# Block attention with top-1 experts on one core: level sums turned, level values kept, rows of x in a line, and gathers in smaller pieces

## The chip, the core and the metric

The kernel runs on one core of a Trainium2 chip. Its engines are TensorE (PE in the profile, with its weight loads as PEld), VectorE (DVE), ScalarE (ACT), GpSimd (POOL) and SyncE (SP), beside 16 DMA engines; each engine works through its own instructions in order. The metric is the time of one execution on the device in microseconds (us); several are taken and their median is given.

## The reference

Attention is computed inside chunks of 64 positions, for 8 batches with 8 heads and 576 positions of 64 values. The heads of a position side by side are a row x of 512 values, which makes 4608 rows ("tokens"). Each token goes to the one expert of eight with the largest gate logit; where an expert has more than `capacity` (80) tokens, those with the highest gate weight are kept; all others give zero.

```python
# q, k, v: (8, 8, 576, 64) float32; w_gate (512, 8); w1 (8, 512, 1024); w2 (8, 1024, 512)
scores = scale * matmul(q_c, k_c.T)              # per chunk of 64 positions
attn = exp(scores - max); attn /= sum + 1e-9
x = matmul(attn, v_c)                            # -> (4608, 512)
logits = x @ w_gate
expert_idx = argmax(logits, axis=1)
gate_w = softmax(logits)[arange(N), expert_idx]
out = zeros((N, D))
for e in range(8):
    tok_idx = where(expert_idx == e)[0]
    if len(tok_idx) > capacity:
        gw = gate_w[tok_idx]
        tok_idx = tok_idx[argpartition(-gw, capacity)[:capacity]]
    h = maximum(x[tok_idx] @ w1[e], 0.0)
    out[tok_idx] = gate_w[tok_idx, None] * (h @ w2[e])
```

## The kernel before

**Attention.** The tokens are 36 tiles (`rt`) of 128. For each, TensorE makes scores, transposes and values, VectorE and ACT the softmax, and x is written by POOL's queue to a scratch in DRAM (`xs`, L486 to L494). The gate's logits follow four tiles at a time.

**Gating.** `gate` (L543) finds the chosen expert as a one-hot row (`comp`, part 0) and the gate weight at that expert (`keys`, 128 tokens x 36 tiles x 8 experts, zero elsewhere). In `parts` POOL adds the token's number in two pieces and its key in three. The capacity's threshold comes from counts: a coarse search (`bounds`, L734) gives each expert a lower bound and a step, and 256 levels stand above it. `levels` (L601) makes (key − bound) × scale and its maximum `bo`, one number for each token; a matrix `lv` of 128 tokens x 256 levels then tells which levels lie under it. ACT makes some of the matrices (`signs`, L618), VectorE and POOL the others (`steps_`, L623). TensorE sums them by expert into `tot` (`total`, L763, `total_last`, L769): the one-hot rows are loaded and 256 columns stream, so `tot` has 8 partitions. `threshold` (L798) counts the levels that reach the capacity (`jkt`, with an accumulator) and turns the count into a threshold for each expert with one float32 matmul (`pn`). The order of the last operations on VectorE is written out by hand as a string, `LAST`: "a" steps tiles 28 to 31, "b" tiles 32 to 35, "c" two matrices on VectorE, "s" two on ACT.

**Slots.** From L1033 on: `mask` compares keys with thresholds, a scan numbers the kept tokens on each partition, TensorE makes their place (`pos`), `hot` (L807) makes a one-hot matrix for each tile (VectorE eight tiles at a time, `pk`, ACT one in nine), and 36 matmuls compact the kept tokens into `cand`. `rank` and `select` (L1080, L1086) order the candidates of each expert on VectorE into 96 slots; `place` (L162) moves row numbers to slots on TensorE. Slots make six rounds of 128 rows, each four groups of 32; a group belongs to one expert. `gic` holds the row numbers as integers, `targets` (L173) the output rows. `keep_warm` (L828) gives TensorE matmuls with no use (`pwarm`) where it has nothing else to do.

**Experts.** `experts` (L189) gathers rounds 0, 1 and 2 from `xs` with POOL (128 rows of 2 KB each), and transposes them on TensorE (`xpose`, L201) with copies by ACT; rounds 3 to 5 are gathered as quarters of rows (`quarters`, L213) and transposed by VectorE (`xpose_blocks`). `layer1` (L230) makes half a round at a time, two groups of 32 matmuls; `layer2` (L248) a round. Weights of 2 MB a layer and expert come on SP's queue; that of expert 3's first layer is held by a VectorE copy from `si` (L1162), the next ones likewise by others (`part`, `ahead`, L1155).

## Time and profile before

| | |
|---|---|
| median of 3 runs | 235.34 us (235.11 to 235.88) |
| the profiled execution's own time | 235.19 us |
| span of that execution | 233.4 us |
| mean granted TensorE clock | 0.993 |
| PE busy | 218.1 us (93 %) |
| DVE busy | 130.5 us (56 %) |
| DMA | 84.81 MB, 363 GB/s |

The profile counts from the start of the span. Attention and the gating that is interleaved with it go on until about 125 us; slots are worked out until 142; expert layers follow to 227, and the last scatter ends it. A row of a timeline tells when a group of equal instructions started, how long it took, and in brackets how long the engine had been idle before and what it had waited for.

### The profile page before, as it was taken

The numbers are of one execution on the slowest core, as the hardware profiler recorded it, in microseconds if no ns is written. First come the engines' busy times: TensorE is split into PE (matmuls) and PEld (weight loads), VectorE is DVE, ScalarE is ACT, GpSimd is POOL, SyncE is SP. The second block draws the span as 40 slices with busy tenths as digits, with TensorE's granted clock in tenths as the row PEclk, the third lists the DMA queues.
The fourth block names the chain that finished last, engine by engine and source line by source line (L and its number), as shares of the span: only waits on it lengthen the run. The fifth ranks groups of instructions, "written<-read, shape, count | busy, mean of one in ns | idle before, by whom it ended". The sixth has DMA issues, their size and how long they took to land. (4 is left out here: it accounts for less than half of the span.)

```text
span 233.4 us, 8196 instructions
## 1 busy us (share of the span) xinstructions
PE 218.1 (93%) x3513; PEld 139.2 (60%) x3513; DVE 130.5 (56%) x411; ACT 73.9 (32%) x161; POOL 66.4 (28%) x145
## 2 busy tenths in 40 slices
PE   7788999999898999999998899999999999999980
PEld 5567787877777787878864555653544536354320
DVE  6678687878779798878878874211131222203110
ACT  3124433343445636566584601321110201101000
POOL 9001203030303019392640823005124060311101
PEclk9999999999999999999999999999999999999997
DMA  6999999999999999998999976999999999999011
GB/s 214 357 406 392 409 422 418 418 421 416 420 411 409 365 409 387 391 405 320 369 437 395 404 274 219 343 423 432 407 406 427 431 409 419 435 421 388 23 46 38
DMA packets 16697, 84.81 MB, mean 363 GB/s; under 512 B 2768, under 2 KB 2896, under 8 KB 12304
## 3 DMA queue, kind: packets, MB, share of 16 engines
q1 hardware_dynamic: 12848, 71.84, 76.6%
q0 software_dynamic: 3664, 12.32, 13.7%
q8 instruction: 30, 0.49, 0.8%
q10 hardware_dynamic: 144, 0.07, 0.1%
q14 instruction: 11, 0.09, 0.1%
HBM read 64.03 MB, written 20.45 MB: 362 GB/s over the span
## 5 line engine op out<-in xcount | busy, mean ns | idle before, releaser
L237 PE MATMUL hc<-w,xtc 128*32 128x256 f32 x768 | 42.8, 379 | 0.2 <-ACT xtc L210 0.2
L254 PE MATMUL yc<-w,htc 128*32 128x512 f32 x384 | 42.1, 592 | 0.0
L406 PE MATMUL s<-kz,qv 128*64 128x128 f32 x544 | 37.2, 279 | 0.9 <-DMA qv<-in_qv 0.9
L237 PEld LDWEIGHTS hc<-w,xtc 128*32 128x32 f32 x768 | 24.7, 110 | 18.3 <-issue 2.4
L442 ACT ACTIVATE pT<-pt 128x512 f32<-128x512 f32 x36 | 21.4, 594 | 36.8 <-PE pt L440 36.7
L406 PEld LDWEIGHTS s<-kz,qv 128*64 128x64 f32 x544 | 29.0, 136 | 6.6 <-issue 6.1
L422 DVE TENSOR_REDUCE mx<-s 128x8 f32<-128x512 f32 (+1 forms) x37 | 24.9, 674 | 11.7 <-PE s L406 11.5
L254 PEld LDWEIGHTS yc<-w,htc 128*32 128x32 f32 x384 | 12.5, 110 | 26.6 <-issue 25.7
L465 PEld LDWEIGHTS o<-qv,pT 64*64 64x64 f32 x1120 | 19.9, 134 | 13.1 <-issue 9.8
L242 ACT ACTIVATE hsc<-hc 128x512 f32<-128x512 f32 x12 | 7.2, 597 | 62.9 <-PE hc L237 62.9
L465 PE MATMUL o<-qv,pT 64*64 64x65 f32 x1120 | 24.9, 224 | 2.2 <-DMA qv<-in_qv 1.1
L244 DVE STREAM_TRANSPOSE htc<-hsc 128x512 f32<-128x512 f32 x12 | 8.5, 711 | 30.1 <-ACT hsc L242 30.1
L259 DVE TENSOR_SCALAR ysc<-yc,gatec 128x512 f32<-128x512 f32 x6 | 4.5, 751 | 36.5 <-PE yc L254 27.4
L424 DVE TENSOR_TENSOR sm<-s,mx 128x512 f32<-128x512 f32 (+1 forms) x37 | 24.7, 668 | 0.1
L484 DVE TENSOR_TENSOR x<-o,rc 128x512 f32<-128x512 f32 x35 | 24.1, 690 | 0.8
L440 PE MATMUL pt<-ct,sm 128*128 128x128 f32 x144 | 23.5, 286 | 0.1
L502 PE MATMUL px<-ct,x 128*128 128x128 f32 x136 | 20.5, 273 | 0.0
L503 ACT COPY xT<-px 128x512 f32<-128x512 f32 x32 | 18.6, 580 | 0.0
L580 POOL TENSOR_TENSOR comp<-comp,ct 128x32 bf16<-128x32 bf16 x18 | 3.9, 237 | 50.4 <-DVE rc L479 40.8
L440 PEld LDWEIGHTS pt<-ct,sm 128*128 128x128 f32 x144 | 15.2, 141 | 2.7 <-DVE sm L424 0.3
L502 PEld LDWEIGHTS px<-ct,x 128*128 128x128 f32 x136 | 15.9, 141 | 0.8 <-issue 0.8
L263 POOL DMA_INDIRECT out<-ysc,si x6 | 6.0, 997 | 30.9 <-DVE ysc L259 20.2
(205 smaller groups left out, 230.9 us busy)
## 6 DMA issues: line engine op xcount, KB each, us to landing
w<-in_w SPq DMA_DIRECT2D x12, 2048.0 KB, 21.7
qv<-in_qv SPq DMA_DIRECT2D x14, 1032.0 KB, 10.6
kz<-in_kh SPq DMA_DIRECT2D x34, 256.0 KB, 10.3
xs<-x POOLq DMA_DIRECT2D x8, 1024.0 KB, 11.0
w<-in_w SPq DMA_DIRECT2D x8, 1024.0 KB, 7.8
out<-zero SPq DMA_DIRECT2D x8, 1024.0 KB, 29.0
qv<-in_qv SPq DMA_DIRECT2D x2, 520.0 KB, 9.6
qv<-in_qv SPq DMA_DIRECT2D x2, 516.0 KB, 9.4
```

The costliest lines, as they stand in the source:

```text
L237: nc.tensor.matmul(h[32 * c:32 * c + 32, j, :], lhsT=xT[r][:, g, b, :], rhs=w[:, b, 256 * c:256 * c + 256], start=(b == 0), stop=(b == 3), ...
L244: nc.vector.transpose(t.rearrange("p j b n -> p (j b n)"), a)
L254: nc.tensor.matmul(y[o:o + 32, :], lhsT=hT[r, g // 2][:, g % 2, c, :], rhs=getw(groups[r][g])[1][:, c, :], start=(c == 0), stop=(c == 7), ...
L406: nc.tensor.matmul(o, lhsT=a, rhs=b, start=True, stop=True)
L422: nc.vector.tensor_reduce(m8, s8, axis=AX.X, op=ALU.max)
L424: d['sub'] = lambda: nc.vector.tensor_tensor(d8, s8, to, op=ALU.subtract)
L440: nc.tensor.transpose(pt[:, pr, :], sv[:, pr, :], ident)
L442: nc.scalar.activation(pT, pt, AF.Exp, scale=0.125)
L465: nc.tensor.matmul(po[h][64 * u:64 * u + 64, 65 * pr:65 * pr + 65], lhsT=d['pT'][64 * h:64 * h + 64, pr, 64 * u:64 * u + 64], rhs=TT[T, r] ...
L484: nc.vector.tensor_tensor(x8, pov[..., 0:64], to, op=ALU.mult)
L502: nc.tensor.transpose(pm[:, pr, :], t['x'][:, r, P * pr:P * pr + P], ident)
L503: copy(t['xT'][:, :, P * r:P * r + P], pm)
```

## The change

1. **Turned sums.** `tot` now has 128 levels on the partitions: each matrix `lv` is loaded in two halves and the 8 columns of the one-hot rows stream. The compare in `threshold` is 16 wide, and its result goes through two bf16 matmuls with ones: the number of levels reached, on every partition. The POOL operations that prepared the scale, and `cnt` and `scale`, are gone.
2. **Kept level values.** (key − bound) × scale is kept for all tiles (`bva`, ordered by expert, then tile), and the mask compares these with the counted level. For the last four tiles `bo` is made from the gate weight and two sums over the one-hot row, beside the key. Matrix 28 moves to ACT and 30 to POOL.
3. **Rows in a line.** Row 128 × tile + partition of `xs`; the last four tiles write with four transfers instead of eight. `targets` turns the number into the output's row with more VectorE operations and stands behind `giq`.
4. **One-hots.** VectorE's steps have 8, 8, 8, 4 and 4 tiles, with four tiles on ACT; the buffers come from other tags, and no warm-up stands behind the last group.
5. **First gather.** Rank, selection and placing of round 0 in two halves of 64 rows, two gathers, and two sets of transposes, the second between the first two groups of layer 1. The gate on the first layer's weights of expert 3 is a POOL memset behind the gather of round 1.
6. **Round 2** is gathered in quarters and transposed by VectorE (`NQ` is 2).

On VectorE, the end of gating, from the matrix of tile 28 (L625) to the mask, before:

```order
L625 TENSOR_SCALAR lv_2494<-io_b,bo 128x256
L593 TENSOR_REDUCE mw_2456<-wt_2453 128x4
L625 TENSOR_SCALAR lv_2497<-io_b,bo 128x256
L594 TENSOR_TENSOR comp<-wt_2453,mw_2456 128x4x8
L596 TENSOR_REDUCE gg_2457<-ex_89 128x4
L597 RECIPROCAL gg_2457<-gg_2457 128x4
L571 TENSOR_TENSOR keys<-comp,gg_2457 128x32
L610 TENSOR_TENSOR bv_2503<-keys,lob 128x32
L613 TENSOR_TENSOR bv_2503<-bv_2503,inw 128x32
L615 TENSOR_REDUCE bo<-bv_2503 128x4
L625 TENSOR_SCALAR lv_2516<-io_b,bo 128x256
```

The same place after:

```order
L636 TENSOR_REDUCE mw_2444<-wt_2441 128x4
L637 TENSOR_TENSOR comp<-wt_2441,mw_2444 128x4x8
L639 TENSOR_REDUCE gg_2445<-ex_87 128x4
L640 TENSOR_TENSOR sw<-comp,ofs 128x64
L643 RECIPROCAL gg_2445<-gg_2445 128x4
L644 TENSOR_REDUCE s_2447<-sw 128x8
L610 TENSOR_TENSOR keys<-comp,gg_2445 128x32
L646 TENSOR_TENSOR gm_2443<-gg_2445,s_2447 128x4
L647 TENSOR_TENSOR bva<-keys,low 128x4x8
L649 TENSOR_TENSOR bo<-gm_2443,s_2447 128x4
L650 TENSOR_TENSOR bva<-bva,ofs 128x4x8
L687 TENSOR_SCALAR lv_2521<-io_b,bo 128x256
```

Two matrices have left the chain, and `bo` no longer comes from the level values.

On VectorE, the first ranks (`bt`, with `rk`), selections and row numbers (`gic`), before:

```order
L1074 TENSOR_REDUCE kc<-s_112 128x8
L1082 SCALAR_TENSOR_TENSOR bt_2648,rk<-kr_2636,kc,ct 128x128
L1082 SCALAR_TENSOR_TENSOR bt_2650,rk<-kr_2636,kc,ct 128x128
L1088 TENSOR_SCALAR sel_2652<-io_b,rk 128x96
L1088 TENSOR_SCALAR sel_2654<-io_b,rk 128x96
L1082 SCALAR_TENSOR_TENSOR bt_2656,rk<-kr_2639,kc,ct 128x128
L170 TENSOR_REDUCE gic_2663<-pl_2658 128x1
L1082 SCALAR_TENSOR_TENSOR bt_2668,rk<-kr_2639,kc,ct 128x128
L1088 TENSOR_SCALAR sel_2670<-io_b,rk 128x96
```

And after:

```order
L1137 TENSOR_REDUCE kc<-s_110 128x8
L1145 SCALAR_TENSOR_TENSOR bt_2659,rk<-kr_2647,kc,ct 128x128
L1151 TENSOR_SCALAR sel_2661<-io_b,rk 128x96
L1177 TENSOR_REDUCE gic_2664<-pl_2663 64x1
L1145 SCALAR_TENSOR_TENSOR bt_2668,rk<-kr_2647,kc,ct 128x128
L1151 TENSOR_SCALAR sel_2670<-io_b,rk 128x96
L1177 TENSOR_REDUCE gic_2664<-pl_2663 64x1
L1145 SCALAR_TENSOR_TENSOR bt_2677,rk<-kr_2650,kc,ct 128x128
L1145 SCALAR_TENSOR_TENSOR bt_2682,rk<-kr_2650,kc,ct 128x128
L1151 TENSOR_SCALAR sel_2684<-io_b,rk 128x96
```

One reduce over placed rows now stands behind each of the first two selections, ahead of the next rank.

On TensorE, from the last spread matmul to the first layer, before (`xpc`, transposes of a gathered round; `hc`, layer 1):

```order
L1126 MATMUL acc<-parts_2712,spread 128x6
L833 MATMUL pwarm<-ct 128x512
L208 MATMUL xpc_0_2793<-ct,xgc_2774 128x128 x2
L208 MATMUL xpc_2_2797<-ct,xgc_2774 128x128 x2
L237 MATMUL hc_0_2801<-w_0_491,xtc_2792 32x256 x32
L208 MATMUL xpc_0_2839<-ct,xgc_2778 128x128 x4
L237 MATMUL hc_1_2845<-w_0_491,xtc_2792 32x256 x16
```

And after:

```order
L1200 MATMUL acc<-parts_2726,spread 128x8
L899 MATMUL pwarm<-ct 128x512
L225 MATMUL xpc0a<-ct,xgc0a 128x64 x4
L270 MATMUL hc_0_2836<-w_0_487,xtc_2829 32x256 x16
L225 MATMUL xpc0b<-ct,xgc0b 128x64 x4
L270 MATMUL hc_0_2836<-w_0_487,xtc_2829 32x256 x16
L270 MATMUL hc_1_2879<-w_0_487,xtc_2829 32x256 x16
L238 MATMUL xpc_0_2897<-ct,xgc_2802 128x128 x4
```

The first transposes have half the columns, the second half of them stands behind the first group of layer 1, and those of round 1 behind the third group.

The diff, cut to what is spoken of:

```diff
-NQ = 3
+NQ = 2
+STORE = 3
...
-LAST = "aaaaaabababasbcbcbbbbbbb"
+LAST = "aaaaaabababasbbbbbbbbbbbb"
...
+        def gather_half(h):
+            t = pool.tile([P, DM], F32, name=f"xg{tag}0{'ab'[h]}", tag="xg", bufs=4)[0:64]
+            nc.gpsimd.indirect_dma_start(
+                out=t, out_offset=None, in_=xs[:, :],
+                in_offset=bass.IndirectOffsetOnAxis(ap=gi(0)[0:64, h:h + 1], axis=0),
+                bounds_check=NT * 512 - 1, oob_is_err=False)
+            xg[0, h] = t
+
+        def xpose_half(h):
+            if h == 0:
+                xT[0] = pool.tile([P, 4, P], F32, name=f"xt{tag}0", tag="xt").rearrange(
+                    "p b (g t) -> p g b t", g=4)
+            pm = pp.tile([P, 4, 64], F32, name=f"xp{tag}0{'ab'[h]}", tag="hp" if h else "xp",
+                         bufs=2 if h else 1)
+            for b in range(4):
+                nc.tensor.transpose(
+                    pm[:, b, :], xg[0, h].rearrange("p (m b) -> p b m", b=4)[:, b],
+                    ident[0:64, 0:64])
+            nc.scalar.copy(xT[0][:, 2 * h:2 * h + 2].rearrange("p g b t -> p b g t"),
+                           pm.rearrange("p b (g t) -> p b g t", g=2))
...
-        for r in range(NQ if extra else 2):
-            gather(r)
         if extra:
+            gather_half(0)
+            gather_half(1)
+            gather(1)
+            extra(-1, xg)
+            quarters(2, None)
             extra(0, xg)
-        xpose(0)
+            xpose_half(0)
+        else:
+            gather(0)
+            gather(1)
+            xpose(0)
         for r in range(NR + 1):
+            start = extra and r == 0
             if r < NR:
-                layer1(r, 0)
-            if r + 1 < (NQ if extra else NR):
+                layer1(r, 0, (lambda: xpose_half(1)) if start else None)
+            if r + 1 < NR and not extra:
                 xpose(r + 1)
             if r < NR:
-                layer1(r, 1)
+                layer1(r, 1, (lambda: xpose(1)) if start else None)
             if extra and NQ <= r + 1 < NR:
                 xpose_blocks(r + 1)
-            if extra and NQ <= r + 2 < NR:
+            if extra and NQ < r + 2 < NR:
...
-                for c in range(2):
-                    r0 = (2 * r + c) * 576 + 512
-                    nc.gpsimd.dma_start(xs[r0:r0 + 64, :], t['x'][64 * c:64 * c + 64, r, :])
+                nc.gpsimd.dma_start(xs[P * i:P * i + P, :], t['x'][:, r, :])
...
+            if rt == RT - 4:
...
+                        lambda: v.tensor_reduce(g, ex, axis=AX.X, op=ALU.add),
+                        lambda: v.tensor_tensor(
+                            sw, oh[:, :, None, :].to_broadcast([P, n, 2, NE]),
+                            ofs[:, None].to_broadcast([P, n, 2, NE]), op=ALU.mult),
+                        lambda: v.reciprocal(g, g),
+                        lambda: v.tensor_reduce(s2, sw, axis=AX.X, op=ALU.add),
+                        key,
+                        lambda: v.tensor_tensor(m, g, s2[:, :, 0], op=ALU.mult),
+                        lambda: v.tensor_tensor(b, kk, low[:, None, :].to_broadcast(bc),
+                                                op=ALU.subtract),
+                        lambda: v.tensor_tensor(bo[:, sl], m, s2[:, :, 1], op=ALU.subtract),
+                        lambda: v.tensor_tensor(b, b, ofs[:, None, 0].to_broadcast(bc),
+                                                op=ALU.mult)):
+                    queue.append((fn, ()))
+                return
             for fn in (
...
-            tot = S['tot'] = ps1.tile([NE, 2 * P], F32, name="tot", tag="pt")
-            nc.tensor.matmul(tot, lhsT=sums, rhs=S['acc'], start=True, stop=False)
-            nc.tensor.matmul(tot, lhsT=nsign, rhs=ones_b[:, 0:1].to_broadcast([P, 2 * P]),
+            tot = S['tot'] = ps1.tile([P, 2, NE], F32, name="tot", tag="pt")
+            for h in range(2):
+                nc.tensor.matmul(tot[:, h], lhsT=S['acc'][:, P * h:P * h + P], rhs=sums,
+                                 start=h == 0, stop=False)
+            nc.tensor.matmul(tot, lhsT=ones_b, rhs=nsign[:, None, :].to_broadcast([P, 2, NE]),
                              start=False, stop=False)
...
-                nc.tensor.matmul(S['tot'], lhsT=comp[:, j, 0], rhs=U[j]['lv'],
-                                 start=False, stop=j == RT - 1)
+                for h in range(2):
+                    nc.tensor.matmul(S['tot'][:, h], lhsT=U[j]['lv'][:, P * h:P * h + P],
+                                     rhs=comp[:, j, 0], start=False,
+                                     stop=h == 1 and j == RT - 1)
...
-            jk = gk.tile([P, 2 * P], BF16, name="jkt", tag="lv", bufs=LV)
-            nc.vector.tensor_scalar(jk[0:NE], S['tot'], capc[0:NE], None, op0=ALU.is_ge,
-                                    op1=ALU.add, accum_out=cnt[0:NE])
+            ge = gk.tile([P, 2, NE], BF16, name="ge", tag="ge", bufs=1)
+            nc.vector.tensor_scalar(ge, S['tot'], capc, None, op0=ALU.is_ge)
             pn = ps2.tile([P, NE], F32, name="pn", tag="g")
-            nc.tensor.matmul(pn, lhsT=cnt.to_broadcast([40, P]), rhs=scale, start=True, stop=True)
+            for h in range(2):
+                nc.tensor.matmul(pn, lhsT=ones_b, rhs=ge[:, h], start=h == 0, stop=h == 1)
...
-            for w, rt in (("a", 28), ("b", 32)):
-                levels(tails[w], rt, 4)
+            levels(tails["a"], 28, 4)
             total()
             total_last(range(20, 28))
             keep_warm(3)
-            tails["c"].extend((steps_, (nc.vector, j)) for j in (28, 30))
             for w in LAST:
                 if w == "s":
-                    signs(29)
-                    signs(31)
+                    steps_(nc.gpsimd, 30)
+                    for j in (29, 31, 28):
+                        signs(j)
                 else:
                     step_one(tails[w])
-            total_last((29, 28, 31, 30))
+            total_last((29, 31, 30, 28))
             keep_warm(3)
...
-                mask, keys.rearrange("p r e -> p e r"),
+                mask, bva,
...
-            for b0, others in ((0, "a"), (9, "a"), (18, "a"), (27, "a")):
-                n = 9 - len(others)
+            for b0, n, b1 in ((0, 8, 8), (9, 8, 17), (18, 8, 26), (27, 4, 31), (32, 4, None)):
                 hot(b0, "v", n)
-                for j, way in enumerate(others):
-                    hot(b0 + n + j, way, 1)
-                order += range(b0, b0 + 9)
+                order += range(b0, b0 + n)
+                if b1:
+                    hot(b1, "a", 1)
+                    order.append(b1)
...
-                if rt % 9 == 8:
+                if rt in (8, 17, 26):
...
-            for e in (0, 1):
-                rank(e)
-            for e in (0, 1):
-                select(e)
+            rank(0)
+            select(0)
+            pl0 = ps2.tile([P, 2, 5], F32, name="pl0", tag="g")
+            gi0 = mp.tile([P, 2], I32, name="gic0")
+
+            def place_first(groups, h):
+                for g in groups:
+                    for o, c in ((32 * g, 0), (32 * g - 64, 1))[:1 + h]:
+                        nc.tensor.matmul(pl0[o:o + 32, c], lhsT=sel_part(*divmod(g, 3)),
+                                         rhs=cb[:, :, g // 3], start=True, stop=True,
+                                         tile_position=(0, o))
+                with nc.allow_low_precision(reason="row numbers are whole and far below 2^24"):
+                    nc.vector.tensor_reduce(gi0[0:64, h:h + 1], pl0[0:64, h, 0:2], axis=AX.X,
+                                            op=ALU.add)
+            place_first((0, 1), 0)
+            rank(1)
+            select(1)
+            place_first((2, 3), 1)
             rank(2)
-            pl0, gi0 = place(mp, ps2.tile([P, 1, 5], F32, name="pl0", tag="g"), sel_part, cb, "c", 0, 1)
             keep_warm(18)
...
-            pt = ps2.tile([P, NE], F32, name="ptot", tag="g")
+            pt = ps1.tile([P, NE], F32, name="ptot", tag="pt")
...
+            gate, sv = targets(mp, [(pl0[:, 0:1], gi0[:, 0:1]), (pl1, gi1)], "c")
+            nc.vector.tensor_tensor(sv, sv, slot_oob, op=ALU.add)
+            si = mp.tile([P, NR], I32, name="si")
+            nc.vector.tensor_scalar(fl, fl, 2 * BIG, None, op0=ALU.mult)
+            nc.vector.tensor_scalar(si, sv, fl, None, op0=ALU.add)
...
+                    if after is True:
+                        nc.gpsimd.memset(w[l][:, 0, 0:1], 0.0)
...
-                if r < 5:
+                if r < 0:
+                    part(3, 0, True)
+                    clear(3.5, nc.sync, 2)
+                elif r < 5:
```

## Rows read from the trace of the kernel before

**Rows 1.** Stretches: window, length, busy us (count) by engine, PE clock, DMA share, GB/s

```profile
136.00:142.20 6.20, 5.98 (x48) 2.83 (x46) 5.56 (x42) 0.53 (x3) 2.96 (x3) 1.00 0.48 163
142.20:226.80 84.60, 84.49 (x1160) 38.28 (x1160) 15.80 (x23) 8.62 (x16) 17.84 (x21) 1.00 0.88 358
...
206.00:216.00 10.00, 10.00 (x164) 5.12 (x160) 2.08 (x3) 1.19 (x2) 0.98 (x1) 1.00 0.95 398
216.00:226.80 10.80, 10.75 (x103) 2.99 (x92) 0.75 (x1) 0.00 (x0) 0.98 (x1) 1.00 0.09 33
```

**Rows 2.** Timeline of VectorE, end of the gate: start us, us, engine, line, operation

```profile
125.00 0.18 DVE L593 TENSOR_REDUCE mw<-wt 128x4 f32<-128x32 f32 x1
125.10 0.28 DVE L625 TENSOR_SCALAR lv<-io_b,bo 128x256 bf16<-128x256 bf16 x1
125.29 0.18 DVE L594 TENSOR_TENSOR comp<-wt,mw 128x32 bf16<-128x32 f32 x1
...
126.72 0.68 DVE L625 TENSOR_SCALAR lv<-io_b,bo 128x256 bf16<-128x256 bf16 x3
```

**Rows 3.** Timeline of VectorE, threshold and mask

```profile
127.87 0.47 DVE L801 TENSOR_SCALAR_CACHE_REDUCE jkt<-tot,capc 8x256 bf16<-8x256 f32 x1 [0.47 <-PE tot L776]
...
128.82 0.69 DVE L1035 TENSOR_TENSOR mask<-keys,pn 128x288 bf16<-128x288 f32 x1 [0.48 <-PE pn L804]
```

**Rows 4.** Groups by line and shape: softmax subtraction on VectorE, busy us and mean ns

```profile
L424 DVE TENSOR_TENSOR sm<-s,mx 128x512 f32<-128x512 f32 x35 | 23.9, 682 | 0.1
```

**Rows 5.** Timeline of VectorE and TensorE, one-hots and the last compaction matmuls

```profile
131.24 2.95 DVE L811 TENSOR_TENSOR pk<-io_h,ptok_b 128x1024 bf16<-128x1024 bf16 x4
134.30 0.64 PE L1062 MATMUL s<-comp,pk 128*128 128x40 bf16 x9
```

**Rows 6.** Timeline of VectorE and TensorE, first ranks, selections and places

```profile
135.69 0.35 DVE L1082 SCALAR_TENSOR_TENSOR bt<-kr,kc,ct 128x128 bf16<-128x128 f32 x1 [0.53 <-PE kr L1100]
136.24 0.40 DVE L1088 TENSOR_SCALAR sel<-io_b,rk 128x96 bf16<-128x96 bf16 x2
136.14 0.59 PE L833 MATMUL pwarm<-io_b,ones_b 128*128 128x512 bf16 x2
136.67 0.20 PE L166 MATMUL pl<-cb,sel 128*32 128x5 bf16 x4
136.91 0.16 DVE L170 TENSOR_REDUCE gic<-pl 128x1 int32<-128x2 f32 x1
136.99 0.34 DVE L1082 SCALAR_TENSOR_TENSOR bt<-kr,kc,ct 128x128 bf16<-128x128 f32 x1
137.25 0.24 DVE L1088 TENSOR_SCALAR sel<-io_b,rk 128x96 bf16<-128x96 bf16 x1
```

**Rows 7.** Timeline of all engines, first gather to the first layer 1

```profile
137.36 1.15 POOL L195 DMA_INDIRECT xgc<-xs,gic  x1 [2.97 <-DVE bt L1082]
...
140.34 0.17 PEld L1126 LDWEIGHTS <-spread 128*128 128x128 bf16 x4 [0.25 <-DVE rowc L182]
...
140.98 0.20 PEld L208 LDWEIGHTS xpc<-ct,xgc 128*128 128x128 f32 x1 [0.24 <-DMA xgc<-xs,gic]
...
141.41 0.64 PE L208 MATMUL xpc<-ct,xgc 128*128 128x128 f32 x4
...
141.83 0.65 ACT L210 COPY xtc<-xpc 128x256 f32<-128x256 f32 x2 [1.82 <-PE xpc L208]
...
142.26 3.66 PE L237 MATMUL hc<-w,xtc 128*32 128x256 f32 x64 [0.22 <-ACT xtc L210]
```

**Rows 8.** Timeline of TensorE, transposes inside the first layer 1

```profile
145.85 0.75 PE L208 MATMUL xpc<-ct,xgc 128*128 128x128 f32 x4
```

**Rows 9.** Timeline of POOL, four level matrices, and the last transfer of x

```profile
101.23 4.52 POOL L625 TENSOR_SCALAR lv<-io_b,bo 128x256 bf16<-128x256 bf16 x4
...
128.03 0.53 POOL L489 DMA_DIRECT2D xs<-x  x1 [6.94 <-DMA xs<-x]
```

**Rows 10.** Timeline of TensorE, second layers of the last two rounds

```profile
212.83 13.92 PE L254 MATMUL yc<-w,htc 128*32 128x512 f32 x128
```

More of the change, by code (lines that the diff above doesn't have):

```diff
@@ L1280, in _constants @@
     p = i[:, None]
[L1281 to L1282 removed]
+    row = P * rt + p
     c[:, C_A:C_A + RT] = row // 64 * 64
```

102 lines of the change are left out of this document (55 added, 47 removed).

## The prediction

> **What bounds the kernel now.** I read the table of stretches first. From 142.20 to 226.80 us TensorE is busy for 84.49 of 84.60 us [rows 1]: the expert layers run without a gap, so their end moves only with their start and with what TensorE itself has to do inside. The DMA engines are full beside it (0.88 of the whole stretch, 0.95 from 206 to 216) but nearly done by 216 (0.09 after) [rows 1]. So the time is the start of layer 1, at 142.26 [rows 7], plus TensorE's own work, and a second limit, the weights, lies close behind. What sets 142.26 is the tail of gating, which I followed back from the timelines of VectorE and TensorE: ranks and selections on VectorE, placing, warm-up matmuls, transposes of the gathered rows. Ahead of that stand one-hots bound by TensorE, mask, threshold, last level matrices. In each hop the reader is to see whether the row has an idle time in brackets, and who ended it: where VectorE has none, shorter VectorE work counts; where it waited for TensorE, TensorE's does. All terms below are in us at the start of layer 1, + for earlier and − for later.
>
> **The change, part by part.**
>
> *Last level matrices.* Two of VectorE's matrices (28 and 30) stood inside the chain of the last four tiles: the step from mw to comp has one between and takes 0.29 [rows 2]; the one ahead of it has the other. An independent step takes 0.10 (125.00 to 125.10), and from comp at 125.29 to the matrices at 126.72 stand one such and six dependent ones, so 0.22 each [rows 2]. Without the two matrices it saves 2 × (0.295 − 0.22) = 0.15. Behind the reduce of the exponentials the line was six dependent steps, 1.33; now it is reciprocal, three that don't wait (sum of two columns, key, product), offset, matrix: 3 × 0.22 + 3 × 0.10 = 0.96, so 0.37. Some operations are 64 wide instead of 32, for which I take 0.04 off: **+0.48** (0.30 if TensorE, which has two pairs of load and matmul for each matrix now, is not ready for them, to 0.57). A pair is about 0.07 (nine in 0.64 [rows 5]). Matrix 30 goes to POOL, at 4.52 / 4 = 1.13 [rows 9]: from about 124.9 it is done at 126.0, in time. It would be late by 3 us if POOL still stood blocked until 128.03, as it does by its eighth transfer of x (6.94 idle [rows 9]); with four transfers instead of eight I expect no block.
>
> *Threshold.* From the start of the compare to the mask's start are 128.82 − 127.87 = 0.95 [rows 3], of which 0.47 is a compare over 256 levels on 8 partitions with an accumulator to be read. Now it is 16 elements wide (0.17, as the small operations of rows 2), and two bf16 matmuls follow instead of a float32 one. The mask waits 0.48 behind the compare; a float32 matmul with its load is 0.19 by four in 0.75 [rows 8], this one counts two, partly side by side, so I put 0.29 on it and 0.19 on passing between engines. 0.17 + 0.13 (two pairs) + 0.19 = 0.49: **+0.465** (0.40 to 0.55).
>
> *Mask.* Its 288 elements take 0.685 reading the keys at a stride of 32 bytes [rows 3], while 512 elements take 0.682 in a row [rows 4]. In a row 288 would take 0.38 by share and with a fixed part about 0.45: **+0.235** (0 to 0.25; none if the stride isn't the cause).
> The Trainium skill, "SBUF — State Buffer", section "Door 1: The DMA port swizzle", says that lines have 16 bytes, with two hits a line wanted for full speed, which fits this pair of rows. The same rule speaks against two other edits: the level values are now written at a stride of 144 bytes, and the 4-wide one-hots use half of each 16-byte run. No row of before shows either.
>
> *One-hots.* VectorE makes four of 8 in 2.95, about 0.74 each [rows 5], and TensorE is the one waited for: after the fourth, the last group's nine pairs run 134.30 to 134.94 [rows 5]. The order now is 8, 8, 8, 4, 4 with four from ACT; the last step's matmuls are 4 instead of 9, and the last two of VectorE take half of 0.74 each. Five pairs of 0.07 leave the tail, a second VectorE start (0.1) and a less even spacing enter: **+0.13** (−0.15 if a 4-wide step costs as much as an 8-wide less a little, to +0.2).
>
> *Rank chain.* This is the part that costs. Before, VectorE does two ranks, two selections, a third rank, and only then reads TensorE's first places (136.91), which are ready by then. Now it does rank, selection, a reduce of the first places, rank, selection, a reduce of the second, in that order; it works in order, so each reduce holds the ranks 1 and 2 behind it until TensorE has placed. The selection is written at about 136.32; the placing matmul stands behind two warm-ups at 136.67 [rows 6], as before; reduce at 136.89, rank 1 at 136.97, selection 1 at 137.36 to 137.60, placing 137.63, reduce 137.87, rank 2 at 137.95, rank 3 at 138.22, selection 2 at 138.49 (steps by rows 6: two ranks to the first selection 0.55, so 0.27 each; from a placing matmul to its reduce 0.24; from the reduce to the rank behind it 0.08; 0.39 where a selection waits for its own rank). Before, selection 2 is at 137.25 [rows 6]: −1.235. All later selections, the other places and TensorE's transposes come that much later. Back comes 0.13: the spread matmuls waited 0.25 for VectorE's row sums [rows 7], which the change moves behind. **−1.1** (−0.9 to −1.3).
>
> *First gather in halves.* It promises an earlier layer 1 but doesn't give it: the transposes of its first half stand on TensorE behind the placing of all other rounds, the spread matmuls and the warm-ups (the order rows above show it). Before, the gather had landed by 140.98 and the first transpose ran at 141.41 [rows 7]. From its issue (137.36 [rows 7]) to landing are 3.62; half a issued 1.3 earlier by the gains above lands near 139.7, half b a gather's issue later (1.15), near 140.9. Both before they are read (141.2 and 143.9), so their cost and gain are nothing; the cover is 1.5 and 3 us. From transposes to the first matmul were 142.26 − 141.41 = 0.85; now four half transposes, then one copy that writes half of the rows (0.33 by half of the row of 0.65 [rows 7], and a full wait for it): 1.03. **−0.18** (0 to −0.25).
>
> *Inside the stretch of layer 1.* The four transposes of round 2 leave TensorE (quarters on VectorE): a block of them costs about 0.75 [rows 8], from 145.85, and pushes the next matmuls; the second half's four enter, with 64 columns each: about 0.6. **+0.15** (0 to 0.3).
>
> *Rest.* Seven more operations for target rows go behind the quarter indices and are needed first by a scatter in the third round: nothing. The weight transfer that waited for a late VectorE copy at 142.03 now waits for a POOL memset behind the second gather, near 141.4: it comes 0.7 earlier, which pays for the four gathers of 512-byte rows. The stream of weights ends at about 216 + 0.09 × 10.8 = 217.0 [rows 1]; the one before it, of 2 MB at 398 GB/s, 5.3 earlier at 211.7, and is read at 212.83 [rows 10]. Margin 1.1 us; nothing by itself.
>
> **The sum.** 0.48 + 0.465 + 0.235 + 0.13 − 1.1 − 0.18 = +0.03 at the start of layer 1, and +0.15 inside: **0.18 us faster**. Against the profiled execution's own 235.19 that is 235.01; against the median of the runs shown, 235.34, it is 235.16. I give **235.15**.
>
> **The rivals.** All against the median of 235.34.
> *A, the ranks cost less.* The gains come at their high ends (0.57, 0.55, 0.25, 0.2, 0.3) and the chain loses 0.9, the copy nothing: +0.97, **234.4**. For it: each of those ends is a row's. Against: the order on VectorE leaves no room under −0.9, since both waits on TensorE are in a row.
> *B, strides.* 4-wide steps at the price of the low bound (−0.15 in place of +0.13) and four writes at a stride, each some 0.025 longer in the chain: 0.18 − 0.28 − 0.10 = −0.2, **235.5**. By the rule of the Trainium skill's page named above (the same section) this would be the outcome; the traces so far show strided reads alone.
> *C, the clock falls (slower).* TensorE is idle for 0.22 of 6.20 us before layer 1 [rows 1] and its granted clock is 1.00 in every stretch. Now it is idle 0.78 more between the two halves of placing. If the clock fell to its lower level, 1.2 GHz of 2.4, for the first stretch of layer 1 of 3.66 us [rows 7], that would take 3.66 more: **238.8**. It decides if the granted clock after 137 reads under 1.00. Against: no such fall in the whole trace.
> *D, the halves buy nothing and the gains come low.* That the gather's halves don't do what they are there for is in the forecast already; if also 0.30, 0.40, 0, −0.15, −1.3, −0.25, 0 are the terms, −1.0: **236.3**.
>
> **How the numbers follow.** Forecast (235.15, between 234.7 and 235.6) 0.52; A 0.26; B 0.10; C 0.05; D 0.07. A measurement tells about 0.3%, or 0.7 us, from no change. Faster by more: A's outer half and a little of the forecast's edge, 0.26 in all; slower: C, D and B's edge, 0.15; the same: 0.59. For 8 in 10 the range reaches to A's value and a bit under, and to most of D: 234.2 to 236.1, leaving out C, D's end and A's extreme.
>
> **What would show it.** In the trace after: the compare narrow and mask under 0.5 us; the mask's start about 0.95 earlier and the end of the one-hots 1.2 to 1.4 earlier than before; two waits of VectorE for TensorE of about 0.4 to 0.5 us among the first ranks, which give nearly all of it back; the half transposes right behind warm-ups with no wait for a gather; the first layer-1 matmul within 0.4 of 142.26; layer 1's groups at a granted clock of 1.00. I am wrong if the half gathers are waited for, if POOL still stands blocked at 125 to 128, or if the last layer 2 waits for a weight.

## The result, and the profile after

The changed kernel takes **238.55 us** (median; 238.4 to 239.0) against 235.40 for the kernel before beside it: ratio **1.0135 [1.0105, 1.0165]**, 3.15 us slower. I had forecast 235.15, with 236.1 as the upper end. The profiled execution of the changed kernel took 238.7, its span 236.9.

Five points of the trace place all of it. They are VectorE's last reduce of the one-hots (kc), the selection of expert 2, the first transposes of gathered rows, the first layer 1 and the first layer 2 (that of round 0), each by the start of its row:

| | kc | selection 2 | transposes | layer 1 | layer 2 |
|---|---|---|---|---|---|
| before | 134.98 | 137.25 | 141.41 | 142.26 | 157.74 |
| after | 134.92 | 138.43 | 142.53 | 143.68 | 160.89 |
| later in this step (us) | −0.06 | +1.24 | −0.06 | +0.30 | +1.74 |

The steps add up to 3.16. From there to the last two rounds' second layers nothing more changes: these start at 215.99 instead of 212.83 [rows 10], 3.16 later. The two spans differ by 3.5; the rest lies behind that point. From the first layer 2 to the end of the span there are 75.65 before and 76.00 after, and 75.3 to 76.2 in the fourteen profiled executions of this case, so I read nothing into it.

The page's row of TensorE's clock shows what no stretch of the kernel before has, a dip:

```profile
PEclk9999999999999999999996799999999999999998
```

It lies in the tail of the gate. Stretches of the changed kernel there (columns as in rows 1, the granted clock last but two):

```profile
124.00:126.00 2.00, 1.18 (x27) 0.71 (x24) 1.93 (x16) 1.48 (x4) 1.19 (x2) 0.99 0.92 375
126.00:128.00 2.00, 1.59 (x18) 0.90 (x19) 1.40 (x9) 1.55 (x4) 1.71 (x9) 0.50 1.13 473
128.00:132.00 4.00, 4.00 (x11) 1.59 (x10) 3.15 (x6) 1.84 (x6) 1.62 (x7) 0.50 0.96 403
132.00:136.00 4.00, 3.72 (x48) 3.24 (x47) 1.95 (x7) 1.54 (x6) 0.19 (x1) 0.90 1.02 418
136.00:142.00 6.00, 5.14 (x45) 2.38 (x43) 4.19 (x27) 0.17 (x1) 2.76 (x3) 1.00 0.34 115
```

and the kernel before in the first of them:

```profile
124.00:126.00 2.00, 2.00 (x16) 1.20 (x14) 1.93 (x14) 1.07 (x3) 0.00 (x0) 1.00 0.91 367
```

Read the first number behind the length, TensorE's busy time, and then the clock. From 124 to 126 TensorE was busy throughout before, with matmuls of 256 columns; turned round they have 8 columns, and it is busy for 1.18 of 2.00. One of these matmuls before, and two after, which waited for a matrix of ACT:

```profile
124.84 0.27 PE L776 MATMUL tot<-lv,comp 128*8 128x256 bf16 x1
```

```profile
125.30 0.20 PE L840 MATMUL tot<-comp,lv 128*128 128x8 bf16 x2 [0.55 <-ACT lv L682]
```

From 126 on the clock is at its lower level (0.50), and 0.90 from 132 to 136 puts its return at about 132.8, so 6.8 us at half speed. From 136 on it is 1.00.

VectorE's timeline of the changed kernel, over the tail (start, us, engine, line, operation, and in brackets the idle time ahead and who ended it):

```profile
127.48 0.23 DVE L866 TENSOR_SCALAR ge<-tot,capc 128x16 bf16<-128x16 f32 x1 [0.31 <-PE tot L840]
128.00 0.46 DVE L1098 TENSOR_TENSOR mask<-bva,pn 128x288 bf16<-128x288 f32 x1 [0.28 <-PE pn L869]
130.01 0.46 DVE L1113 TENSOR_REDUCE ptok_b<-s 128x36 bf16<-128x288 f32 x1 [0.71 <-PE s L1107]
134.92 0.18 DVE L1137 TENSOR_REDUCE kc<-s 128x8 f32<-128x24 f32 x1 [1.50 <-PE s L1125]
136.83 0.15 DVE L1177 TENSOR_REDUCE gic<-pl 64x1 int32<-64x2 f32 x1 [0.56 <-PE pl L1173]
137.81 0.15 DVE L1177 TENSOR_REDUCE gic<-pl 64x1 int32<-64x2 f32 x1 [0.28 <-PE pl L1173]
138.43 0.24 DVE L1151 TENSOR_SCALAR sel<-io_b,rk 128x96 bf16<-128x96 bf16 x1
```

The mask starts 0.82 earlier than before (128.00 against 128.82 [rows 3]), yet kc comes at the same time: between them VectorE waits 0.71 and 1.50 for a TensorE at half speed, where it waited 0.37 and 0.80 in the kernel before. The two reduces behind kc wait 0.56 and 0.28, as forecast.

TensorE's timeline of the changed kernel, first layers of round 0:

```profile
142.53 0.69 PE L225 MATMUL xpc0a<-ct,xgc0a 64*128 64x64 f32 x4
143.68 1.93 PE L270 MATMUL hc<-w,xtc 128*32 128x256 f32 x32 [0.46 <-ACT xtc L228]
...
146.16 1.06 PE L270 MATMUL hc<-w,xtc 128*32 128x256 f32 x15
147.38 1.12 PE L270 MATMUL hc<-w,xtc 128*32 128x256 f32 x5 [0.16 <-issue]
148.83 2.80 PE L270 MATMUL hc<-w,xtc 128*32 128x256 f32 x44 [0.33 <-issue]
```

POOL's of the same time:

```profile
143.04 1.00 POOL L249 DMA_INDIRECT xqc<-xs,giq  x1 [0.63 <-DVE gatec L182]
...
146.95 1.00 POOL L249 DMA_INDIRECT xqc<-xs,giq  x1 [0.30 <-issue]
```

No transpose waits for a gather, as forecast. But TensorE stops in the middle of a layer 1, at 146.85 by its last record there; five matmuls come in between, and the next block in a row runs from 148.83. In the kernel before, 64 of these matmuls take 3.66 in one piece [rows 7]. The brackets name no releaser ("issue"): nothing that the profile records held TensorE. What stands beside the stop is POOL, which issues the four quarter gathers of round 2 one after the other. The experiments take up these two things, the clock and the stop.

### The profile page after: what moved, and what is told of

It is laid out like the page before. It is cut to its first block, busy times and chain, and to the rows that moved or that the text cites. A ratio compares the mean times of both kernels' runs of the same rounds, so it can differ in the third digit from the quotient of the medians.

```text
span 236.9 us, 8256 instructions
## 1 busy us (share of the span) xinstructions
PE 221.1 (93%) x3533; PEld 141.7 (60%) x3533; DVE 133.8 (56%) x423; ACT 73.7 (31%) x161; POOL 67.4 (28%) x143
## 5 line engine op out<-in xcount | busy, mean ns | idle before, releaser
L270 PE MATMUL hc<-w,xtc 128*32 128x256 f32 x768 | 44.0, 380 | 1.1 <-issue 0.5
L270 PEld LDWEIGHTS hc<-w,xtc 128*32 128x32 f32 x768 | 25.5, 110 | 19.4 <-issue 4.3
L249 POOL DMA_INDIRECT xqc<-xs,giq x16 | 16.0, 1002 | 6.1 <-issue 4.8
```

The source lines that it names most:

```text
L249: nc.gpsimd.indirect_dma_start(out=t[:, P * g:P * g + P], out_offset=None, in_=xs.rearrange("r (c d) -> (r c) d", c=4), in_offset=bass.Ind ...
L270: nc.tensor.matmul(h[32 * c:32 * c + 32, j, :], lhsT=xT[r][:, g, b, :], rhs=w[:, b, 256 * c:256 * c + 256], start=(b == 0), stop=(b == 3), ...
```

## The experiments

In different profiled executions kc comes up to 0.7 later or earlier than the edits explain, from what happens ahead of it. So beside the medians I compare steps: from kc on, and ahead of it from lg, VectorE's last reduce of the gate's logits, to kc.

### The clock: e1_warm

The changed kernel with more warm-up matmuls in the stretch where the turned sums leave TensorE idle:

```diff
             total_last(range(20, 28))
-            keep_warm(3)
+            keep_warm(12)
...
             total_last((29, 31, 30, 28))
-            keep_warm(3)
+            keep_warm(4)
```

> The changed kernel with more warm-up matmuls in the gate's tail: behind the sums of tiles 20 to 27 one long and two short ones instead of one short, behind those of 28 to 31 two short ones instead of one. Theory: the clock fell at 125.96 because the turned sums leave TensorE idle or with 8-column matmuls there; filled, the granted clock stays at 1.00 until layer 1 and about 1.1 us come back: 237.4 us. Rival: the clock fell for another reason; it falls again near 126 to 128 and the time stays at 238.5. In both, the stall of 1.9 us in the first layer 1 stays, as nothing there is changed.

Measured: 236.98, ratio to before 1.0077 [1.0048, 1.0106]. Its stretches:

```profile
124.00:126.00 2.00, 2.00 (x30) 1.11 (x26) 1.93 (x15) 1.51 (x4) 1.29 (x2) 1.00 0.96 391
126.00:128.00 2.00, 1.60 (x20) 0.83 (x20) 1.42 (x8) 0.51 (x2) 1.71 (x9) 1.00 1.06 438
```

and VectorE's timeline:

```profile
126.39 0.67 DVE L687 TENSOR_SCALAR lv<-io_b,bo 128x256 bf16<-128x256 bf16 x3
127.36 0.23 DVE L866 TENSOR_SCALAR ge<-tot,capc 128x16 bf16<-128x16 f32 x1 [0.30 <-PE tot L840]
127.88 0.46 DVE L1098 TENSOR_TENSOR mask<-bva,pn 128x288 bf16<-128x288 f32 x1 [0.28 <-PE pn L869]
133.78 0.18 DVE L1137 TENSOR_REDUCE kc<-s 128x8 f32<-128x24 f32 x1 [0.80 <-PE s L1125]
```

The clock stays at 1.00 and kc comes at 133.78, 1.14 earlier than in the changed kernel and 1.20 earlier than before. Part of both is only an earlier start. The rows of lg before, in the changed kernel and in e1:

```profile
123.92 0.29 DVE L541 TENSOR_REDUCE lg<-acc 128x32 f32<-128x128 f32 x1 [0.18 <-PE acc L537]
```

```profile
123.73 0.29 DVE L580 TENSOR_REDUCE lg<-acc 128x32 f32<-128x128 f32 x1 [0.19 <-PE acc L576]
```

```profile
123.62 0.29 DVE L580 TENSOR_REDUCE lg<-acc 128x32 f32<-128x128 f32 x1 [0.18 <-PE acc L576]
```

From lg to kc are 11.06 before, 11.19 in the changed kernel and 10.16 in e1. So the gate's edits are worth 0.90 at kc, and the fallen clock took 1.03 back, more than all of it. That the idle time brought the fall, rather than something else in the changed gate, rests on this: filling it, with nothing else edited, kept the clock. The kernels below bear it out: e2 and e3, which do not fill it, have the clock at 0.50 from 128 to 132 too (11.20 and 11.19 from lg to kc), and the nine kernels that fill it have no fall there (10.14 to 10.17). Turned sums alone in the kernel before were not run. The stop in layer 1 stayed here, with the clock at 1.00 (TensorE goes on at 147.67), so the two are separate.

### Halves or quarters: e2_whole and e3_round2

e2 puts the first gather and its ranks back as before and keeps the rest, the quarters of round 2 among it. e3 keeps the halves and gathers round 2 whole, with TensorE's transposes for it.

```diff
# e2_whole
-            gather_half(0)
-            gather_half(1)
+            gather(0)
...
-            rank(0)
-            select(0)
...
+            for e in (0, 1):
+                rank(e)
+            for e in (0, 1):
+                select(e)
# e3_round2
-NQ = 2
+NQ = 3
...
-            quarters(2, None)
+            gather(2)
...
-            if r + 1 < NR and not extra:
+            if r + 1 < NR and (not extra or r == 1):
                 xpose(r + 1)
```

> The changed kernel with the first gather whole as before: ranks 0 and 1, selections 0 and 1, rank 2, one placing, one gather of 128 rows, four transposes of 128 rows ahead of layer 1. Round 2 stays in quarters. Theory one: the halves cost 1.23 us of ranks, 0.3 of copy, and cause the stall of 1.9 us in the first layer 1: 238.55 - 1.23 - 0.3 - 1.9 + 0.6 (half b's transposes leave the layer, the whole ones come in front) = about 235.3, no slow records among the matmuls of the first layer 1. Theory two: the quarters of round 2, four gathers of 512-byte rows at 143 to 148, cause the stall: the ranks alone come back, about 237.0, the stall stays.

> The changed kernel with round 2 gathered whole and transposed by TensorE as before; the first gather stays in halves. Theory one (halves cause the stall): the stall stays, four transposes come back to TensorE (+0.7): about 239.2. Theory two (quarters cause it): the stall goes, 238.55 - 1.9 + 0.7 = about 237.4.

Measured: e2 236.84, 1.0051 [1.0015, 1.0088]; e3 237.20, 1.0066 [1.0039, 1.0093]. TensorE's first layer 1 in e2, then in e3:

```profile
142.34 0.72 PE L238 MATMUL xpc<-ct,xgc 128*128 128x128 f32 x4 [0.86 <-DMA xgc<-xs,gic]
143.28 3.98 PE L270 MATMUL hc<-w,xtc 128*32 128x256 f32 x52 [0.22 <-ACT xtc L240]
147.58 2.80 PE L270 MATMUL hc<-w,xtc 128*32 128x256 f32 x44 [0.33 <-issue]
```

```profile
146.21 3.66 PE L270 MATMUL hc<-w,xtc 128*32 128x256 f32 x64
```

With the halves gone the stop stays; with the quarters under layer 1 gone, the 64 matmuls again take 3.66 in one piece. The quarters make the stop. e2's first row says more: the ranks take their old time again (kc to selection 2 is 2.28, before 2.27), but the transposes then wait 0.86 for the data. Part of that wait is POOL's: it starts the gather at 138.15, 1.03 behind its row numbers, where the kernel before took 0.29; why stays open. So not all of the ranks' 1.24 comes back at layer 1; e4 and e12 below tell how much.

### Everything undone that cost: e4_three and e4_again

e1, e2 and e3 together: the turned sums, kept level values and linear rows stay, with the clock kept, a whole first gather and three whole rounds. e4_again is the same kernel, run beside the last group of experiments.

> The changed kernel with all three undone at once: the first gather whole, round 2 whole, and the warm-ups of e1_warm. What is left of the change are the turned sums, the kept level values, the rows in a line, the one-hots in two steps of four, and the POOL memset. If the gains ahead of the ranks are real and only hidden (0.48 + 0.465 + 0.235 + 0.13 = 1.3 us at the start of layer 1): about 234.1, faster than before. Rival: they are hidden by something else (a wait for the gather, for weights, or a clock that falls all the same), and the time is that of before, 235.3.

> The kernel of e4_three once more, beside e10_split on the same chip. With round 2 transposed by VectorE and no stall, e10_split should be 0.75 us (four transposes of TensorE) below it; if it is not, the transposes were not worth their place. By its first comparison e4_three is at 0.999 of before: 235.2.

Measured: 235.27, 0.9990 [0.9963, 1.0017], and 235.17, 0.9959 [0.9925, 0.9992]. The profile has the first layer 1 0.80 earlier than before in the first (141.46) and 0.30 in the second (141.96). TensorE, e4_again:

```profile
141.01 0.72 PE L238 MATMUL xpc<-ct,xgc 128*128 128x128 f32 x4 [0.70 <-DMA xgc<-xs,gic]
141.96 5.39 PE L270 MATMUL hc<-w,xtc 128*32 128x256 f32 x96 [0.22 <-ACT xtc L240]
```

The gather is now the last to arrive: issued at 136.25, waited for until 141.01, 4.8 us later, where before it took 3.62 [rows 7]. (In e4_three the transposes start at 140.51 with no such wait.) The gate's 0.90 reaches layer 1 only in part: from lg to layer 1 are 18.34 before, 17.67 in e4_three and 18.24 in e4_again. This is the miss of my expectation for e4_three, 234.1: I had carried the whole gain through.

### What the stop needs: e5, e6, e7 and e9

All four have the clock kept. e5 (whole first gather) and e9 (halves, but both selections first and one reduce, and no warm-up ahead of the first transposes) issue no quarters before the loop; round 2's quarters come under the first layer 1 of round 1, behind an ACT result. e6 issues the four quarters directly behind the second gather, ahead of the memset that lets a weight transfer go. e7 issues three quarters instead of four (a quarter of round 2's rows is zero there).

```diff
# e5_later
-            quarters(2, None)
...
-            if extra and NQ < r + 2 < NR:
+            if extra and NQ <= r + 2 < NR:
                 quarters(r + 2, hs[r])
# e6_order
+            quarters(2, None)
             extra(-1, xg)
-            quarters(2, None)
# e7_three_quarters
-            for g in range(4):
+            if r == 2:
+                nc.vector.memset(t[:, 3 * P:], 0.0)
+            for g in range(3 if r == 2 else 4):
# e9_both: e5, and
+            gather_half(0)
+            gather_half(1)
-            gather(0)
...
-            keep_warm(8)
+            keep_warm(0)
```

> As e4_three, but round 2 is gathered in quarters again, paced by the first layer's result of round 0 (issued near 149 instead of 142), and transposed by VectorE. Theory one, the stall belongs to quarters in flight while layer 1 of round 0 runs behind the 2 MB transfer: no stall, TensorE has four transposes (0.75 us) less: 235.27 - 0.75 = about 234.5. Theory two, four gathers in a row on POOL stall TensorE wherever they stand: a stall of 1 to 2 us near 150 to 155, about 236.

> First gather whole, more warm-ups, round 2 in quarters early; the only difference to e2_whole with warm-ups (which should be about 235.8) is that the 2 MB transfer of expert 3's first layer is let go behind the four quarter gathers instead of ahead of them. Theory one, the stall comes from quarters that wait in the DMA queues behind the 2 MB transfer: quarters land within 4 us of their issue, no stall in layer 1; the weights come some 5 us later, and if they are then waited for the time is 237 or more. Theory two, the gathers' issue itself: the stall stays where the fourth one is issued.

> First gather whole, more warm-ups, round 2 in quarters early but only three of the four; the fourth column block is set to zero, so a quarter of round 2 is left out of the computation. If the stall hangs on the fourth gather (it ended 0.8 us behind that one's end in three kernels): no stall, or one that ends 1.3 us earlier, about 234.6. If it hangs on the quarters being outstanding in the queues, or on the place in TensorE's instruction stream: the stall is at the same matmul, about 235.8.

> As e5_later, and the first gather in halves again, but without the waits between the ranks: ranks 0 and 1, selections 0 and 1, rank 2, then all of round 0 is placed and one reduce gives both columns of row numbers. The eight-step warm-up ahead of the first transposes (1.1 us) is left out. If only the order of ranks made the halves costly: half a lands near 139.3, layer 1 starts near 140.5 instead of 141.5 (e4_three), about 233.6. Rivals: the clock falls without that warm-up (+1 or more), or the weights become late (w2 of expert 6 had 1.1 us): 234.5 as e5_later.

Measured: e5 236.22, 1.0021 [0.9987, 1.0056]; e6 235.87, 1.0006 [0.9979, 1.0033]; e7 234.80, 0.9964 [0.9932, 0.9996]; e9 237.30, 1.0075 [1.0035, 1.0116]. TensorE in e5, and behind it the last of POOL's four gathers there:

```profile
147.89 8.25 PE L270 MATMUL hc<-w,xtc 128*32 128x256 f32 x128
156.92 1.97 PE L270 MATMUL hc<-w,xtc 128*32 128x256 f32 x32 [0.78 <-issue]
```

```profile
155.19 1.00 POOL L249 DMA_INDIRECT xqc<-xs,giq  x1 [0.30 <-issue]
```

The same in e6:

```profile
141.98 4.54 PE L270 MATMUL hc<-w,xtc 128*32 128x256 f32 x56 [0.22 <-ACT xtc L240]
146.87 2.40 PE L270 MATMUL hc<-w,xtc 128*32 128x256 f32 x40 [0.35 <-issue]
```

```profile
145.11 1.00 POOL L249 DMA_INDIRECT xqc<-xs,giq  x1 [0.30 <-issue]
```

TensorE in e7:

```profile
143.10 6.07 PE L272 MATMUL hc<-w,xtc 128*32 128x256 f32 x96 [0.22 <-ACT xtc L240]
```

and in e9, the half gather (POOL) and the transposes that read it (TensorE):

```profile
136.41 1.09 POOL L212 DMA_INDIRECT xgc0a<-xs,gic  x1 [2.95 <-DVE bt L1144]
```

```profile
140.54 0.66 PE L225 MATMUL xpc0a<-ct,xgc0a 64*128 64x64 f32 x4 [0.66 <-DMA xgc0a<-xs,gic]
```

The stop goes with the four gathers, 10 us later too (e5, e9), and stays when no weight transfer is queued behind or beside them (e6: from 141 to 147 all that the DMA engines moved were 0.52 MB on the gathers' queue). In each TensorE is back 0.72 to 0.88 us behind the end of the last gather's issue: 147.95 and 148.83 in the changed kernel, 156.19 and 156.92 in e5, 146.11 and 146.87 in e6. With three gathers the 96 matmuls take 6.07 instead of 5.39: by their starts there is one gap of 0.42, and TensorE is back at 145.92, 0.74 behind the end of the third gather (145.18). So the stop follows the end of the row that POOL issues, and a shorter row makes a shorter stop. e9 missed its 233.6 for two reasons: it has the stop (its layer 1 stretch is 17.53), and the half that was issued at 136.41 was still waited for until 140.54, no sooner than the whole gather of e4_three was read (140.51). The clock stayed at 1.00 without the warm-up.

### Two and two, and the kernel before with four: e10, e11, e12

If the length of the row decides, two gathers, a pause and two more must be free (e10: whole first gather, clock kept), and the kernel before must get a stop from four gathers moved under a layer 1 (e11). e12 is the changed kernel with the clock kept and the gathers two and two, so its halves stay alone as a cost.

```diff
# e10_split, e12_mended
-            quarters(2, None)
...
             if r < NR:
                 layer1(r, 0)
+            if start:
+                quarters(2, hs[0], range(0, 2))
...
                 layer1(r, 1, (lambda: xpose(1)) if start else None)
+            if start:
+                quarters(2, hs[0], range(2, 4))
# e11_before_early: the kernel before, and
+            if extra and r == 0:
+                quarters(3, hs[0])
```

> As e5_later, but the four quarter gathers of round 2 are issued two and two: two behind the first half of layer 1 of round 0 (near 146), two behind the second (near 150). Theory: TensorE gets no further instructions while POOL issues indirect gathers in a row, and has a stock of some 150 of them; in six kernels its stall ended 0.72 to 0.76 us behind the last of a row of four (5.0 us), with three in a row it was 0.4 us. Two in a row (2.3 us) fit into the stock: no stall, layer 2 of round 0 near 156.5, 234.7. Rival: it is the sum of gathers under layer 1 that counts, not a row of them: a stall at either place, 235.5 or more.

> The kernel before, with one thing moved: the four quarter gathers of round 3 are paced by layer 1 of round 0 instead of round 1, so they are issued near 150 to 156 under layer 1 instead of near 158 to 163 under layer 2 (one buffer more for it). Theory: the stall can be made in the kernel before, too: TensorE runs dry near 154 and goes on 0.7 us behind the fourth gather, near 157, some 1.5 us lost, 236.8. Rival: the stall needs something of the change: no gap, 235.3.

> The changed kernel with the first gather in halves and its order of ranks left as they are, but with the warm-ups of e1_warm and the quarters two and two as in e10_split. Against e10_split it tells the price of the halves alone. Theory: 1.23 us of ranks and 0.2 of copy at the start of layer 1, and 0.6 of transposes in it: 2.0 us more than e10_split, 236.7. Rival: the earlier gather of the half gives some of it back: less than 1 us more.

Measured: e10 **234.82, 0.9952 [0.9916, 0.9989]**; e11 236.89, 1.0053 [1.0011, 1.0096]; e12 236.12, 0.9999 [0.9965, 1.0033]. TensorE in e10 and then POOL (in its profiled execution the clock was at half for 3.4 us in the attention, so all its times are later than they would be: kc by 0.8 to 1.6 against the other kernels that keep the clock):

```profile
143.25 5.39 PE L271 MATMUL hc<-w,xtc 128*32 128x256 f32 x96 [0.22 <-ACT xtc L240]
...
149.24 8.86 PE L271 MATMUL hc<-w,xtc 128*32 128x256 f32 x159
```

```profile
148.35 1.02 POOL L251 DMA_INDIRECT xqc<-xs,giq  x1 [0.53 <-DVE htc L278]
149.67 1.00 POOL L251 DMA_INDIRECT xqc<-xs,giq  x1 [0.30 <-issue]
152.77 1.02 POOL L251 DMA_INDIRECT xqc<-xs,giq  x1 [0.53 <-issue]
154.09 1.00 POOL L251 DMA_INDIRECT xqc<-xs,giq  x1 [0.30 <-issue]
```

TensorE in e11, and the first and the last of POOL's four gathers:

```profile
154.33 1.06 PE L237 MATMUL hc<-w,xtc 128*32 128x256 f32 x15
156.10 1.09 PE L237 MATMUL hc<-w,xtc 128*32 128x256 f32 x6 [0.70 <-issue]
157.52 2.58 PE L237 MATMUL hc<-w,xtc 128*32 128x256 f32 x42 [0.33 <-issue]
```

```profile
151.71 1.03 POOL L218 DMA_INDIRECT xqc<-xs,giq  x1 [0.53 <-DVE htc L244]
...
155.65 1.00 POOL L218 DMA_INDIRECT xqc<-xs,giq  x1 [0.30 <-issue]
```

The same four gathers cost nothing in e10 (159 matmuls in one piece of 8.86) and the kernel before gets the stop as soon as it issues four in a row under a layer 1. Its own four stand under a layer 2 and cost nothing there: TensorE goes through 32 second-layer matmuls in the time of 64 first-layer ones.

e12 against e10 prices the halves. From kc to layer 2 e12 takes 24.17 and e10 22.56: 1.24 for the ranks, less 0.61 because e10's transposes then wait for their gather, 0.22 for the copy, 0.76 inside layer 1 (most of it the second half's transposes, which push the matmuls by 0.62). The medians differ by 1.30, where I had expected 2.0: the gather's arrival hides half of what the ranks cost. e10 against e4_again, whose difference is round 2's transposes off TensorE: 22.56 and 23.55 from kc to layer 2; the medians (234.82 and 235.17) are 0.35 apart, within their scatter. So **e10 is the version to keep**: its median is the lowest of all kernels that leave nothing out, and from lg to the first layer 2 it takes 32.72, against 33.82 in the kernel before. Its 0.5% against the kernel before is less firm than its interval: in this comparison the median of before was 235.90, in the earlier ones 235.31 to 235.48, and the kernel of e4 came out 0.4% faster here and 0.1% there.

## Why the prediction was wrong

Step by step, in its own order:

- **Last level matrices**, +0.48 forecast: +0.03. The matrices come 0.33 earlier in e1 (126.39 against 126.72 [rows 2]), but lg comes 0.30 earlier too: from lg to them are 2.80 before and 2.77 in e1. I had counted six steps behind the reduce of the exponentials; the order after lists nine (one on sw and two on bva more). They take 1.24 in e1 (125.15 to 126.39) instead of the forecast 0.96, against 1.33 before. POOL's matrix is done at 125.95 in the changed kernel, in time as forecast. Not forecast was that TensorE's sums end sooner: from the matrices to the compare are 0.97 in e1 and 1.15 before, +0.18.
- **Threshold and mask**, +0.465 and +0.235: from compare to mask 0.52 (127.36 to 127.88) instead of 0.95, so +0.43; the mask takes 0.46 instead of 0.685, +0.23. Both held, though the scan behind the mask takes 0.08 more (0.84 against 0.76).
- **One-hots**, +0.13: from ptok_b to kc 4.20 in e1 (129.58 to 133.78) instead of 4.31, +0.11. Held. Of rival B's prices one was there, and it did not decide: the strided level values of earlier tiles take 0.20 to 0.22 where the same operations took 0.18 to 0.19, so 0.02 to 0.03 each, as B had it. (In the last four tiles they take 0.27 and 0.28, but with the same strides, so the stride is not what makes those longer.) The 4-wide one-hots take 0.42 and 0.55 against 0.68 to 0.82 for 8: half of that is 0.34 to 0.41, and a fixed part, such as the 0.17 of small operations, would make up the rest as well, so that the half line costs anything is not shown. The Trainium skill, "SBUF — State Buffer", section "Door 1: The DMA port swizzle", with its lines of 16 bytes, agrees in two places: the mask read in a row gains, and the strided write loses a little.
- **Rank chain**, −1.235: +1.24 later. Exact, with the two waits at the reduces. Taken back, it gives only 0.63 at the transposes, because they then wait for their gather (e12 against e10).
- **Spread matmuls**, +0.13 back: not seen. From selection 2 to the transposes are 4.10 after and 4.38 in e1, before 4.16.
- **Halves**: no transpose waits for them in the changed kernel, as forecast. **Copy**, −0.18: −0.30 (transposes to layer 1 1.15 against 0.85).
- **Inside layer 1**, +0.15: without the stop +0.07 (15.41 in e12, 15.48 before).

Two steps failed outright. The first is the step that was not made: I read the granted clock as 1.00 throughout the trace of before and asked only whether the new waits behind 137 could lower it. The threshold and level terms took TensorE's work away in a stretch where it was what kept the clock up, and I counted that work at nothing. It cost 1.03. Rival C named 238.8, near the result, but its place (behind 137) and price (3.66 in layer 1) were not what happened; by its own test, the clock behind 137, it is refuted, and its figure came near by luck.

The second is the last line of the change's parts, "which pays for the four gathers of 512-byte rows". I priced the quarters as bytes on the DMA queues. Their price is on TensorE: 17.22 − 15.41 = 1.81 in layer 1. Nothing in the trace of before showed it, but its quarters stood under a layer 2, and the change puts them under a layer 1. I costed that move at nothing without naming the row that would bound it; it should have had a bound and a rival. (The weight transfer that was to come 0.7 earlier and pay for them is issued at 142.44 instead of 142.21, late like all else.)

With both mended, e12 is the change as I had costed it: 0.9999 [0.9965, 1.0033], where the forecast was 0.18 us faster. The two that I had missed, 1.03 and 1.81, are 2.84 of the 3.3 us between the forecast and the result. Most of the rest is the term of the level matrices, 0.45 too large: the gate's edits were to give 1.31 and give 0.90. So even without the two the sum would have missed its sign by the trace: from lg to the first layer 2 e12 takes 34.32, the kernel before 33.82.

## What to carry to other kernels

Work that is made smaller on an engine whose clock follows its activity has to be checked at that place: list TensorE's busy time in the stretch before and after, and fill it if it drops. A gather costs more than its bytes: beside a stretch of short matmuls where TensorE is the bound, as this layer 1, issue indirect gathers in ones or twos and not four in a row (under layer 2 four cost nothing here). And a step that advances one stage's issue (the halves) is worth only what the next arrival allows; look for the transfer that lands last before paying VectorE time for it.

## What the runs showed of the hardware that I had not expected

**A row of indirect gathers holds TensorE.** Loads and matmuls counted together by their starts, between the start of the first gather of a row and the stop (the first gap; e7 is the kernel with three gathers):

| kernel | first gather starts | last one ends | TensorE stops | goes on | records between |
|---|---|---|---|---|---|
| after | 143.04 | 147.95 | 146.85 | 148.83 | 102 |
| e1 | 142.00 | 146.91 | 145.97 | 147.67 | 102 |
| e2 | 141.92 | 146.84 | 145.69 | 147.58 | 101 |
| e6 | 141.21 | 146.11 | 144.38 | 146.87 | 96 |
| e5 | 151.26 | 156.19 | 153.76 | 156.92 | 92 |
| e9 | 151.80 | 156.73 | 154.29 | 157.45 | 91 |
| e11 | 151.71 | 156.65 | 155.02 | 157.52 | 98 |
| e7 | 141.57 | 145.18 | 145.50 | 145.92 | 96 |

TensorE gets through 91 to 102 more instructions (not the 150 of e10's expectation) and then has only small groups of them, 10 to 33 in all with four gathers, until 0.72 to 0.88 us behind the last gather, as if its instructions were not supplied while the gathers are issued. Two and two gave no gap. Under a layer 2 the 5 us of four gathers cover 88 to 96 records, and no kernel has a stop there; but e7's three cover 90 and have one, so the count alone does not decide it. A late transfer of instructions is not what ends the stop: in the changed kernel the queues that the page calls "instruction" move no packet from 142.0 to 152.9. Through what the gathers hold TensorE stays open: no run separated the count of gathers from the length of the row in time.

**A first gather that is issued early is on its way for longer.** From issue to the transposes that wait for it are 3.62 in the kernel before [rows 7], 4.8 in e4_again, 4.3 in e6 (136.70 to 141.03), 4.6 in e10 (137.71 to 142.31), and 4.1 for 64 rows in e9. But it does not hold for every execution: e4_three's, issued at 136.32, was read from 140.51 on without a wait, and the halves of the changed kernel and of e12, issued at 137.27 and 136.87, landed 2.9 later. What it queues behind was not tried.
